# A top-k attention and two-layer MoE kernel: w3 @ w_out multiplied in float32 from decoded blocks, the order settled anew with later landings

## The chip, the cores and the metric

The kernel runs on 1 core of one Trainium2 chip. The metric is the device time in microseconds (us) of one execution. Engines are named as the profile names them: PE (TensorE; PEld its weight loads), DVE (VectorE), ACT (ScalarE), POOL (GpSimd), SP (SyncE, which issues the DMAs).

## The reference

```
# attention: q, k, v are (4, 8, 576, 64) float32, top_k = 32
scores = q @ k.T / 8
kth    = 32nd largest of each row; scores below it -> -1e9
attn   = exp(scores - max); attn /= sum(attn) + 1e-9
x      = (attn @ v), heads put side by side          # (2304, 512)
# moe: w_in (512, 2048), w_out (2048, 512)
h = x @ w_in;  x = (h * sigmoid(1.702 h)) @ w_out
# moe2: w1, w2 (512, 1024), w3 (1024, 1024), w_out (1024, 512)
out = ((x @ w1) * (x @ w2) @ w3) @ w_out             # (2304, 512) float32
```

The six weights reach the kernel as float64. Since nothing stands between `@ w3` and the last `@ w_out`, the kernel multiplies these two weights with each other once and applies the product, which it calls w34.

## The kernel before

The 2304 tokens are 18 tiles of 128; 18 tiles by 8 heads are 144 heads, counted here from 0.

**Weights (`weights`, L799).** A float64 weight arrives in 72 blocks of 128x512 elements (512 KB each). `load64` (L469) decodes each into a float32 block: one instruction on ACT or POOL for the low bits (L488 or L515), one for sign (L498 or L493), one on ACT into a PSUM bank (L503), one on DVE that joins them (L507). The landing buffer is free again when L503 has read it. `l2_scale` (L538) takes the norm of a group of blocks (four small matmuls per block, L551, and a few one-column instructions). `split` (L591) makes of a scaled block two float16 halves, hi and lo, since products are done as three float16 matmuls, hi*hi, hi*lo and lo*hi (`product_op`, L782: lines L789, L790, L791; 128x512 each).

**w34.** The moe2 w_out is 8 blocks (E4), w3 is 16 (E3). E4's blocks are split like others (hi: L598 ACT, L601 DVE or L604 POOL; lo: through PE L607 and DVE L614, through PE L610 and L611 and ACT L617, or on POOL L626 and L627). Each block of w3 is turned by PE and split by `split_turned` (L674), in one of two ways that the plan chooses: four float32 matmuls against a scaled identity (L681), hi on ACT (L691), a matmul that takes hi off the bank (L697), lo on ACT (L700); or four float32 transposes (L688), hi on ACT (L691), lo on DVE (L703). For each of the 8 output blocks then follow 24 float16 matmuls from two blocks of w3, and the result is itself split: hi L825 (ACT) or L828 (DVE), lo L832 (DVE) or L837 and L840.

**Tiles.** A head is a score matmul S (L1127), four rounds of MAX8 (L1147) and three of MATCH_REPLACE8 (L1150) on DVE, a cut out of PSUM (L1165) and an exponential (L1168) on ACT, a split into halves (ACT or POOL L1174, L1228; POOL L1177, L1180), a DMA transpose, and attn @ v on PE (L1195, L1199). A tile ends in the two MoE layers, which are products of `product_op` with the evictions between them. w34 is first used at the end of tile 0's MoE.

**Order.** Every step is an `Op` with one or more alternatives (engine, estimated cost). The order in which all ops are written, and the alternative of each, comes from a table, `PLAN`, found beforehand; `Order.run` (L76) goes through the ops in that order, gives each its buffers (pools of PSUM banks, SBUF blocks and slots) and records the instruction. So each engine's queue, SP's included, is fixed by the table, and each engine takes its queue strictly in order. The costs in the code (`lat=`, numbers beside "A", "V", "G", "T") are the estimates with which the table was found; they delay nothing on the chip.

Of the kernel before, what the change touches and what calls it, by code (L numbers as in the profile page):

```python
# [21 lines left out]
P = 128  # L22
C = 512
# [14 lines left out]
class Order:  # L38
    GAP = {"T": 0.25, "V": 0.16, "A": 0.16, "G": 0.1, "D": 0.05, "N": 0.0}
    SAME = {"T": 0.0, "V": 0.12, "A": 0.12, "G": 0.1, "D": 0.25, "N": 0.0}  # L40
    DMA = 2.1
    COLD = ((50.0, 1.28), (100.0, 1.03))
# [33 lines left out]
    def run(self, log=None):  # L76
        free = dict.fromkeys("TVAGD", 0.0)
        lock = moved = 0.0
        for o in sorted(self.ops, key=lambda o: o.rank):
# [21 lines left out]
            if e == "G" or (e == "V" and fn in self.both):  # L101
                cost += max(lock - now, 0.0)
                lock = now + cost
            o.eng, o.start = e, now
            free[e] = o.end = now + cost
            if e == "D":
                moved = max(moved, now + 0.3) + o.data
                o.end = max(o.end, moved) + o.lat
            for name, env, key in o.rel:
# [32 lines left out]
    'c-jq@W1A(t0!2$nC8?w;N!3{A^f^6k_t-N%wr$(CZQHhO+qP}%oqPYm{;;3D)>af%(G{rJN@^vG;`8~HJW5_AzhWpr!3t5h!jv>hCdKomQUXe>66Oo_rBgzb'  # L142
    'cqKteRthWCl{!iRUqN4zl3U5A6jLhu8u{Az+WAT<6@9yv`btA(lrmMB>-*)~9C9>dy0Th1t6WhYDKC|`zE{d`<&W}3`R6OBwpaQp!<CWB4CTJ>r*DLRoU&ZG'
    'p*&VzD_@l#itVrEpXiVG=T<MMoz#WuGIhDST0QJP;TIuK)lYt;2%l73CB2eX$>7WEi%_DJvPuPCC0}i&sZvxa?yI6yRaz+-m8`ySU!0Od(G=5X`KaP3)s&jP'
    'TE1pVS0$)K`l5X~l_E+<Wr%O6Z<exEX{~he4OYe~)0DbOJ*9!tMCqZ-QRXXqlmp5^rKd99w@^8*oKRXQEq&dULCR!hnX<vR$+uV8ubfoQD;JcD%4OxMa?O`j'
    '4Oe5;C&~-o2Srh#`d!gg<R@x6)l!+C`xDh1Y6-Qb+DL7owp7!oq5cRpuUbsaqQ>|W{JGS!YH_u^zn;H|+EgvAlvg?^os@1$FQvEAPZ^*LR7NOclnKgAWuvmC'
    '!J!668cZy>NLjD!R3<6sd{caveDeyfQPwK!l)D8#DxZ{Z%It#Ml*P(+Wu<aU*{s}FR`^ym*wJ8DgMG>|<&1J&xvAVy?kNwHhssmsx$;JNr@U8&s1wwc>Kb*e'
    'x=vlMZculthtyN*dG(t5Ks8mVW>N!coSIWr{YD|z@A>nn`P9;C8MU0MsaO?iDz%haM-BSJ)M$Spe`~da+D+}Fj#6v;>#Ftrjs5-Afoev-uaMs#;vcHcP?xAn'
    ')y-;Ge~&`F{bT*d)Jy7ob%nZBy`p|o|EQX#Ylim5|5p9%|LTv_qBNxO!ct48<<|;mr9vu(R1V3ig%{4IW!GA0Z8fa9nx_S{f!ZK#lr~<Qs+9|=rd1EA6*5;_'
    't<BVC7hbF_*S2a0wL{ti?U7bTYg4#`)>nI|ebzQ<I}7jC4roZnx~)5U27QmZ-+$15S-q-8soDJb)rx90wXNFD-&q~4PFMS?1JvQ_ICYkKR6Xv$qyANiHb@<;'  # L150
    'j#1~T^VCV|Wd9ETUiGxvOl|IO@9(H~QKzVj{2SGq>PPjgde{HT|3Uqw{#H%R3Q4O4wG3JoEli8ia%vCNcj`~o)*Nk^I?_L0y{_I+Q)wAPVzp!~ueLy2sI3Xv'
    'rk&Rwsn68s>I?Oys%WYPwbWX)mZ@;lM!rUq8<p0|Hfq?YNuxA{>kX<sXxN}cEl;DQMl~Cq)y`>`w9DER?Va{s`=}{8(RDp3;0E#q78O~puhKW`S@bwPR?ng5'
    '*GmRU1*!+0YrnML+JD+Vjq9GCUJvRqdP0!`fn0&wfuZ_ZeYU<%57l$)QF=i=LeHy5>P2*^r_wX(ne;F{Tu;=q={fa6dR@Jx-a+rASJfNpZS=PKM15mmQeab{'
    'T#@>L%7F%fP%R>)Q%F~>x7J+i9MUbMpEg08rp*bNAF@>2s1??VYIQ@}Y3;RqTA`34S_!R^R$ptN^$!`WjnPJEW3}laGqhP+cdduE=l{iF`VsAv_C@=vnfi9^'
    'SjerAXWAQWnYJQieaLR@q;^<49&$qarm6a4Ekq9lD(Thqi(2+TdA+9IT(75h)cXed=`;18TC+eeeXu@9Z?AXOyXal@Zh8;BzdleOrH|9c>l5^8`Ye5}K3`v~'
    'uh!S->-DYrZvBjYF>obtBk;ONY%nocDELax5KI@$8r-X&&=2S*^#^(`BiYDp9MMk)jt1@ruIYCIw*yZD--;MUMx&rn+Ncw(9jq5TR^*|6PJgM>lt{xd;*32-'
    '{slnL3cf2+ESM=+Hh8GWt;RPSKWf~^m|*lZCL2mh(V!hH9xSY<1R4bz>%H|?TD*Q%zpFpf%j&HHWArWhWqp7?Jg_0~RsW;=jOs>1qq)(}$ZTXWqKpzo1>>Wh'
    'BUm?B-)LmS80C$o!Olh(qn|O%m}<;578{L?iNQI>d}E8T$XF8G9^7H<G}ag!f*Xz9#vbF0@zcP7fk^PtaDfNXfb1X|WCJ-tE>IZc1^GgYf>NLY_@w{VRYNm`'
    'A&sCBW<(hAMowc?$_it&vB_v=bO^Qz_6jB$C5<9RDI<SMxnQMWm0(X}s4?6aX^b<b81syk#yVrGamjd|@-O9Oidyt~${XW_@!dFUJPh6qJ_;T-t^|(+uLbuT'
    '$Bc8vW#fi%&v<6MHr^XwjUUGE6a$z*fNv=PARs}OqTx-$n&ximFB%e>H8dhL36uooKxI%B)CCPd3(y9120cM9FboU_6TlvD1zZK+!8ULN90g~<U@!`d0W-iz'  # L160
    'FdfVR%fNE54y@3x>cmK8ECl<&NpKy!0B-?-Hsmlf%nHlETCgD;u1(Rp>m&53fsuhh!D+$&bQtUdc4+&w>)K82o_0UvPe|Ip+mLjD1S1HNL4HsG)C^q{>SnDE'
    '(q+vHr|UEHZTb%Vp#C{9FgQ3^E3{7NeW;qyw9L3L9+oOBb(n3sVUgxu^N@MgykuT8KZJb@`xJKFycrf@7BNei70ile<*-^|wZrP0EyFsR$IPeZEAzeiJxmKv'
    'D3PPYe`a#{4>JW-K@Ct3^eWtlU=fYbmhj%VFdB<4qlf4b`Vd~WWV@0Y<`L%+#x_oiE92G??IZd{B;n+UsW=fozzzu|QIV06MI(zxMw8W%`^kB7gWM!fB5y@1'
    'Q9Yx+M$)K$RuikMHO^XKowAlj@#y){ccVl!uv{z5O0r5=&7)dGjgLx>8Wgp}I%#F1L7GgfNAHe47X3cDI4v8!gl?rr=y7_UhQ-W^nIH3*K8e21Hq)mxD~n)p'
    'tXfR<m|ZcgSi6{ttS0No2C#uKW^Db~-m%Gc#n|okRi@asoz^a9SC4HHdoVU=uZ^ANEO3@MOPxc`vAE-Lr{b15C*s~XvAj4h$;<Id@y+8q#P^Nw!3W1*cCI`3'
# [24 lines left out]
    'BXM?|8<&iz5K$|l3GRiP;{kXC9)-u_X?Q38iGyT1o`aX*jU|`kJ@^aONlr2sAH>J;IeY@AA>~PP(u-Wcm+%dIyX15H83W>y#w3o!lLDkW=|cvP$z&#(MHZ07'  # L190
    'WG&f6j*tsvJ$XQ$l5gZ0c}Knz$I4`7vGQ7RR!*ykRn^);xRqd~SgowFR$Hr&HQU;3ZL@Y;pRMX<KXbS_Dr|Y!mavEBWV8gWMoZBSv>WX~d(m-p72QNH!oQ#&'
# [1376 lines left out]
```

## Time and profile before

| | before |
|---|---|
| device time, median of 3 | 990.6 us (990.5 to 991.75) |
| the profiled execution's own time | 994.35 us |
| its span, first to last instruction | 992.6 us |
| PE, DVE, ACT, POOL busy | 942.2, 901.7, 730.0, 832.5 us |
| mean granted TensorE clock | 0.988 of 2.4 GHz |

The profiled execution is 3.75 us above the median of the runs, and its span 2.0 us above. Spans and shares below are of the profiled execution. A matmul's record lasts from its issue to its modelled end, so records of matmuls that follow each other overlap, and PE's pace is read from the starts.

### The profile page before, as it was taken

The numbers are of one execution on the slowest core, as the hardware profiler recorded it, in microseconds if no ns is written. First come the engines' busy times: TensorE is split into PE (matmuls) and PEld (weight loads), VectorE is DVE, ScalarE is ACT, GpSimd is POOL, SyncE is SP. The second block draws the span as 40 slices with busy tenths as digits, with TensorE's granted clock in tenths as the row PEclk, the third lists the DMA queues.
The fourth block names the chain that finished last, engine by engine and source line by source line (L and its number), as shares of the span: only waits on it lengthen the run. The fifth ranks groups of instructions, "written<-read, shape, count | busy, mean of one in ns | idle before, by whom it ended". The sixth has DMA issues, their size and how long they took to land. (4 is left out here: it accounts for less than half of the span.)

```text
span 992.6 us, 20241 instructions
## 1 busy us (share of the span) xinstructions
PE 942.2 (95%) x6790; PEld 495.7 (50%) x6790; DVE 901.7 (91%) x1939; ACT 730.0 (74%) x1369; POOL 832.5 (84%) x1180
## 2 busy tenths in 40 slices
PE   5688879899999999999999999999999999999998
PEld 2445544445455555545555555545455555555544
DVE  6999999899999999999999999999999999999422
ACT  7999989896877787877688776776785775646241
POOL 6889999898899999999999999988897878757142
PEclk9699999999999999999999999999999999999999
DMA  9999988876788887767887868669666667555401
GB/s 322 291 280 291 277 179 191 173 135 131 122 149 151 155 156 136 134 130 152 146 158 139 147 129 147 121 127 165 127 126 134 113 118 117 111 90 102 99 11 33
DMA packets 398569, 149.37 MB, mean 150 GB/s; under 512 B 376576, under 2 KB 384768, under 8 KB 398464
## 3 DMA queue, kind: packets, MB, share of 16 engines
q1 hardware_dynamic: 398464, 148.07, 72.3%
q8 instruction: 53, 0.87, 0.4%
q14 instruction: 52, 0.43, 0.1%
HBM read 52.43 MB, written 4.72 MB: 58 GB/s over the span
## 5 line engine op out<-in xcount | busy, mean ns | idle before, releaser
L1147 DVE MAX8 m8s<-ysb 128x8 f32<-128x576 f32 x432 | 320.5, 752 | 5.7
L1150 DVE MATCH_REPLACE8 ysb<-m8s,ysb 128x576 f32<-128x576 f32 x288 | 213.6, 742 | 0.0
L1180 POOL TENSOR_TENSOR ysb<-ysb 128x512 f16<-128x512 f32 x141 | 163.8, 1166 | 0.3
L1165 ACT ACTIVATE ysb<-s_ps,m8s 128x576 f32<-128x576 f32 x144 | 106.7, 741 | 77.5 <-DVE m8s L1147 72.5
L789 PE MATMUL mm<-w,usb 128*128 128x512 f16 x388 | 147.1, 379 | 1.2 <-POOL usb L1319 1.0
L791 PE MATMUL mm<-w,usb 128*128 128x512 f16 x388 | 147.0, 379 | 0.0
L790 PE MATMUL mm<-w,usb 128*128 128x512 f16 x388 | 147.0, 379 | 0.0
L791 PEld LDWEIGHTS <-usb 128*128 128x128 f16 x912 | 89.1, 98 | 107.8
L789 PEld LDWEIGHTS <-usb 128*128 128x128 f16 x912 | 89.0, 98 | 100.2 <-issue 7.0
L1168 ACT ACTIVATE ysb<-ysb,nbs,asm 128x576 f32<-128x576 f32 x144 | 124.5, 867 | 17.0 <-DVE nbs L1157 8.5
L790 PEld LDWEIGHTS <-usb 128*128 128x128 f16 x912 | 89.1, 98 | 91.3 <-issue 2.1
L789 PE MATMUL mm<-wout,usb 128*128 128x512 f16 x304 | 115.3, 379 | 1.7 <-DMA usb<-usb 0.6
L791 PE MATMUL mm<-wout,usb 128*128 128x512 f16 x304 | 115.2, 379 | 0.0
L790 PE MATMUL mm<-wout,usb 128*128 128x512 f16 x304 | 115.2, 379 | 0.0
L1147 DVE MAX8 m8s<-s_ps 128x8 f32<-128x576 f32 x144 | 108.6, 754 | 6.2 <-PE s_ps L1127 3.4
L1150 DVE MATCH_REPLACE8 ysb<-m8s,s_ps 128x576 f32<-128x576 f32 x144 | 107.5, 747 | 0.0
L1127 PE MATMUL s_ps<-kts,qts 128*128 128x288 f16 (+1 forms) x640 | 96.4, 290 | 2.5 <-ACT ysb L1165 2.2
L789 PE MATMUL mm<-win,usb 128*128 128x512 f16 x220 | 83.5, 379 | 0.6 <-DMA usb<-usb 0.6
L791 PE MATMUL mm<-win,usb 128*128 128x512 f16 x220 | 83.4, 379 | 0.0
L790 PE MATMUL mm<-win,usb 128*128 128x512 f16 x220 | 83.4, 379 | 0.0
L1195 PE MATMUL mm<-v2s,ats 128*128 128x65 f16 (+1 forms) x1440 | 79.1, 194 | 3.4 <-DMA ats<-ysb 2.7
L1195 PEld LDWEIGHTS <-ats 128*128 128x128 f16 (+1 forms) x1440 | 73.5, 100 | 12.4 <-DMA ats<-ysb 3.8
(369 smaller groups left out, 2131.3 us busy)
## 6 DMA issues: line engine op xcount, KB each, us to landing
w<-in_moe_w_out_dram SPq DMA_DIRECT2D x24, 512.0 KB, 5.5
w<-in_moe_w_dram SPq DMA_DIRECT2D x22, 512.0 KB, 5.7
w<-in_moe_w_in_dram SPq DMA_DIRECT2D x16, 512.0 KB, 6.0
qts<-qts SPq DMA_DIRECT2D x34, 128.0 KB, 2.6
out_dram<-usb SPq DMA_DIRECT2D x17, 256.0 KB, 2.3
usb<-in_q_dram SPq DMA_DIRECT2D x15, 256.0 KB, 3.4
usb<-in_v_dram SPq DMA_DIRECT2D x11, 256.0 KB, 3.1
usb<-in_k_dram SPq DMA_DIRECT2D x10, 256.0 KB, 3.3
```

The lines of the kernel that those rows point to most:

```text
L789: nc.tensor.matmul(o, a[:, i, :], hi, start=(first and i == 0), stop=False)
L790: nc.tensor.matmul(o, a[:, i, :], lo, start=False, stop=False)
L791: nc.tensor.matmul(o, a[:, 4 + i, :], hi, start=False, stop=(last and i == 3))
L1127: nc.tensor.matmul(E["sp"][r : r + n, i], qe[q_][:, h, r : r + n], kt[:, j, i * HS : (i + 1) * HS], start=k_ == 0, stop=k_ == 1,)
L1147: nc.vector.max(out=E["m8"][:, 8 * i : 8 * i + 8], in_=E["sp"] if i == 0 else E["w"])
L1150: nc.vector.match_replace(out=two(E["w"]) if i == 0 else E["w"], in_to_replace=E["m8"][:, 8 * i : 8 * i + 8], in_values=E["sp"] if i == 0 ...
L1165: nc.scalar.activation(two(E["y"]), E["sp"], AF.Prelu, bias=E["m8"][:, TOPK - 1 : TOPK], scale=-1.0, alpha=1.0 / FAR)
L1168: nc.scalar.activation(E["y"], E["y"], AF.Exp, bias=E["nb"], scale=nesc)
L1180: return lambda: eng.tensor_tensor(hl()[:, S + SR : 2 * S], E["y"][:, 0:SM], hl()[:, 0:SM], op=ALU.subtract)
L1195: nc.tensor.matmul(heads_av()[r : r + n, j_, 0 : D + 1], at_, v2[:, j_, blk, D : P + 1], start=(i == 0), stop=(i == 8),)
```

## The change

Three parts.

1. E4's 8 blocks are no longer split, and the 16 blocks of w3 no longer halved. A block of w3 is turned by four float32 transposes and copied from PSUM to SBUF as float32 (`turned3`); w34 is 8 float32 matmuls of 128x512 per output block, 64 in all, straight from decoded blocks. The scales, which were in the halves, go into the eviction of the result (`by`, two columns of a new `s34`).
2. The split of w34's result has the scale as a column, and its lo may be made on POOL.
3. The estimates in the planner are changed: DMA landings later (`lat=`), POOL instructions a little dearer, a price for DVE instructions that share with POOL, and a limit on DMA work under way at a DMA transpose. A new `PLAN` was found with them: the order and the alternatives of the whole program are others.

```diff
+    def turned3(W, E):
+        bank = lambda: E["mm"]
         def f_in():
-            E["by"] = -1.0
-            for i in range(4):
-                nc.tensor.matmul(
-                    bank()[:, i], W["w"][:, i * P : (i + 1) * P], turned, start=i == 0, stop=False, skip_group_check=True
-                )
...
+            for i in range(0, C, P):
+                nc.tensor.transpose(E["mm"][:, i : i + P], W["w"][:, i : i + P], ident)
+        def f_a():
+            nc.scalar.copy(E["f"], E["mm"])
...
+        a = pe(0.45, 0.0, f_in, deps=[W["join"], W["gram"]], env=E, acq=["f", "mm"], rel=[("blk", W, "w")], tag="w3 in")
+        return op([("A", 0.48, f_a, 0.0), ("V", 0.6, f_v, 0.0)], 0.0, deps=[a], env=E, rel=["mm"], tag="w3 turned")
...
-        i4, s4, d4 = l2_scale(E4, quarter(0))
-        sp4 = [split(E, s4, d4) for E in E4]
-        g3 = [l2_scale(E3[8 * g : 8 * g + 8], quarter(1 + g)) for g in range(2)]
+        i4, s4, d4 = l2_scale(E4)
+        g3 = [l2_scale(E3[8 * g : 8 * g + 8]) for g in range(2)]
+        s34 = wcols(2)
...
-                tr = split_turned(W, g3[f // 4][1], e)
-                last = product_op(
-                    0.0, lambda E=E: E["mm"], lambda e=e: e["t"], E4, [4 * kc + i for i in range(4)],
-                    kc == 0, kc == 1, [tr, last, pr] + sp4[4 * kc : 4 * kc + 4], [("mm", E, "mm")] if kc == 0 else [], rel, "w34",
-                )
+                tr = turned3(E3[2 * f + kc], e)
+                for i in (0, 2):
+                    def f_w34(E=E, e=e, i=i, kc=kc):
+                        for n in (i, i + 1):
+                            nc.tensor.matmul(
+                                E["mm"], e["f"][:, n * P : (n + 1) * P], E4[4 * kc + n]["w"],
+                                start=kc == 0 and n == 0, stop=kc == 1 and n == 3,
+                            )
...
-                nc.scalar.activation(halves(E["o"])[0], E["mm"], AF.Copy, scale=G34)
+                nc.scalar.activation(halves(E["o"])[0], E["mm"], AF.Copy, scale=by)
...
-        ld = dma(0.5, due - 20, f_load, env=E, acq=keys, tag="w load", lat=2.5, data=1.62)
+        ld = dma(0.5, due - 20, f_load, env=E, acq=keys, tag="w load", lat=2.9, data=1.62)
...
-            tr = [dma(1.35, due + 8, f_t, deps=[lo], env=E, acq=["at"], rel=["hl"], tag="a T", lat=1.6, data=1.42, after=last_of.get("a T"))]
+            tr = [dma(1.35, due + 8, f_t, deps=[lo], env=E, acq=["at"], rel=["hl"], tag="a T", lat=2.2, data=1.42, after=last_of.get("a T"))]
```

PE's queue where w3 is first turned. Names: `mm` are PSUM banks, `wout` and `win` hold decoded weight blocks here, `usb` the halves or copies of turned w3, `s_ps` the scores. Before, behind the S of head 3:

```order
L688 MATMUL mm_96<-ident,wout 128x128 x4
L681 MATMUL mm_97<-tsb,wout 128x128 x4
L681 MATMUL mm_95<-tsb,wout 128x128 x4
L697 LDWEIGHTS ident
L697 MATMUL mm_97<-usb,ident 128x512
L688 MATMUL mm_96<-ident,wout 128x128 x4
L697 LDWEIGHTS ident
L697 MATMUL mm_95<-usb,ident 128x512
L688 MATMUL mm_97<-ident,wout 128x128 x4
L789 LDWEIGHTS usb
L789 MATMUL mm_95<-wout,usb 128x512
```

In the changed kernel the first float32 products (L815), just ahead of the S of head 4, with the transposes (L690) of a later block between them (`wout` and the `w_` tiles are blocks of E4 and E3):

```order
L815 MATMUL mm_94<-w_71,usb 128x512 x2
L690 MATMUL mm_93<-ident,wout 128x128 x4
L577 LDWEIGHTS ones
L577 MATMUL mm_95<-wsm,ones 128x1
L994 LDWEIGHTS ones
L994 MATMUL mm_96<-kvc,ones 128x1
L995 LDWEIGHTS ones
L995 MATMUL mm_96<-kvc,ones 128x1
L815 MATMUL mm_94<-w_71,usb 128x512
L815 MATMUL mm_94<-wout,usb 128x512
L815 MATMUL mm_94<-w_70,usb 128x512 x2
```

The take-off matmuls L697 are gone, products come in long float32 matmuls, and other work of PE stands between those of one output block.

ACT's queue at the same stage, before (L691 and L700 are hi and lo of w3, L503 and L498 decode later blocks, L1168 is a head's exponential):

```order
L691 ACTIVATE usb<-mm_96,wsm 128x512
L1168 ACTIVATE ysb<-ysb,nbs,asm 128x576
L691 ACTIVATE usb<-mm_97 128x512
L503 ACTIVATE mm_98<-w_72 128x512
L691 ACTIVATE usb<-mm_95 128x512
L700 ACTIVATE usb<-mm_97 128x512
L691 ACTIVATE usb<-mm_96,wsm 128x512
L700 ACTIVATE usb<-mm_95 128x512
L498 ACTIVATE win<-w_72 128x512
```

and in the changed kernel (L693 is the copy of a turned block; L513, L508, L498 decode; L1174, L1180 and L1171 are a head's exponential, hi and cut):

```order
L1174 ACTIVATE ysb<-ysb,nbs,asm 128x576
L693 COPY usb<-mm_94 128x512
L990 ACTIVATE usb,kvc<-wout,nbs 128x8x64
L991 ACTIVATE kr_82,kvc<-rest,nbs 64x2x64
L693 COPY usb<-mm_93 128x512
L693 COPY usb<-mm_96 128x512
L513 ACTIVATE mm_96<-w_70 128x512
L420 ACTIVATE usb<-wout,kvc 128x8x64
L1180 CAST ysb<-ysb 128x576
```

One copy per block stands where one or two instructions stood.

## Rows read from the trace of the kernel before

**Rows 1.** The page: busy us of each engine, share, instructions.
```profile
PE 942.2 (95%) x6790; PEld 495.7 (50%) x6790; DVE 901.7 (91%) x1939; ACT 730.0 (74%) x1369; POOL 832.5 (84%) x1180
```

**Rows 2.** Windows: us, busy of each engine, granted clock, DMA share, GB/s.
```profile
core 0: us, PE busy (x) PEld busy (x) DVE busy (x) ACT busy (x) POOL busy (x), PEclk, DMA share, GB/s
0.00:200.00 200.00, 161.09 (x1109) 90.36 (x1110) 181.28 (x412) 183.68 (x352) 176.39 (x264) 0.94 0.93 251
200.00:225.00 25.00, 24.02 (x169) 12.31 (x169) 25.00 (x62) 23.50 (x45) 22.78 (x34) 1.00 0.71 130
225.00:992.60 767.60, 757.08 (x5515) 393.07 (x5512) 695.44 (x1467) 522.86 (x974) 633.36 (x884) 1.00 0.68 125
```

**Rows 3.** The same view in stretches of 25 us.
```profile
25.00:50.00 25.00, 16.14 (x107) 11.02 (x105) 24.06 (x57) 22.85 (x48) 21.67 (x32) 0.67 1.00 291
50.00:75.00 25.00, 21.90 (x136) 11.80 (x135) 24.17 (x50) 24.41 (x45) 22.04 (x33) 1.00 0.94 281
75.00:100.00 25.00, 22.76 (x162) 13.78 (x162) 24.93 (x56) 25.00 (x46) 23.43 (x35) 1.00 1.00 292
100.00:125.00 25.00, 21.85 (x175) 13.03 (x173) 23.75 (x54) 24.09 (x48) 23.96 (x35) 1.00 1.06 274
```

**Rows 4.** Waits of the DMA queue (SP), 50 to 100 us, then 100 to 200 us.
```profile
SPq L483 <- ACT mm L503: 17.3, 14, 3.7
...
SPq L483 <- ACT mm L503: 15.0, 9, 3.9
```

**Rows 5.** PE's timeline: start us, us, instruction.
```profile
43.93 0.60 PE L688 MATMUL mm<-ident,wout 128*128 128x128 f32 x4
45.20 2.02 PE L681 MATMUL mm<-tsb,wout 128*128 128x128 f32 x16 [0.66 <-POOL nbs L1157]
...
50.67 0.38 PE L789 MATMUL mm<-wout,usb 128*128 128x512 f16 x1 [0.40 <-ACT usb L700]
50.88 0.38 PE L790 MATMUL mm<-wout,usb 128*128 128x512 f16 x1
51.10 0.38 PE L791 MATMUL mm<-wout,usb 128*128 128x512 f16 x1
...
212.79 1.02 PE L652 MATMUL mm<-win,tsb 128*128 128x512 f32 x2
213.64 1.02 PE L652 MATMUL mm<-w,tsb 128*128 128x512 f32 x2
...
225.08 0.65 PE L1127 MATMUL s_ps<-kts,qts 128*128 128x288 f16 x4
```

**Rows 6.** Groups of ACT, then DVE: shapes, count | busy us, mean ns.
```profile
L1464 ACT COPY usb<-mm 128x512 f32<-128x512 f32 x25 | 14.4, 577 | 10.6 <-PE mm L791 10.3 <-POOL usb L1319 0.3
L700 ACT ACTIVATE usb<-mm 128x512 f16<-128x512 f32 x9 | 5.5, 613 | 0.0
L691 ACT ACTIVATE usb<-mm 128x512 f16<-128x512 f32 x9 | 5.4, 620 | 0.0
L691 ACT ACTIVATE usb<-mm,wsm 128x512 f16<-128x512 f32 x7 | 4.9, 693 | 0.0
...
L703 DVE SCALAR_TENSOR_TENSOR usb<-mm,wsm,usb 128x512 f16<-128x512 f32 x7 | 5.1, 733 | 0.0
L832 DVE SCALAR_TENSOR_TENSOR win<-mm,win 128x512 f16<-128x512 f32 x3 | 2.0, 673 | 0.0
```

**Rows 7.** Single lines up to 75 us, E4's splits: min/median/max ns.
```profile
L601 DVE TENSOR_SCALAR wout<-w,wsm x1: 1077/1077/1077, 32.5 to 32.5; 128x512 f16<-128x512 f32 x1
...
L604 POOL TENSOR_SCALAR wout<-w,wsm x3: 694/697/698, 30.1 to 31.8; 128x512 f16<-128x512 f32 x3
...
L614 DVE SCALAR_TENSOR_TENSOR wout<-w,wsm,mm x4: 730/734/747, 34.2 to 41.5; 128x512 f16<-128x512 f32 x4
...
L627 POOL TENSOR_TENSOR wout<-w,wout x2: 1159/1162/1165, 34.9 to 36.9; 128x512 f16<-128x512 f32 x2
```

**Rows 8.** One line of ACT in the first 45 us, the same columns.
```profile
L598 ACT ACTIVATE wout<-w,wsm x3: 710/712/722, 29.2 to 33.3; 128x512 f16<-128x512 f32 x3
```

More of the change, by code (lines that the diff above doesn't have):

```diff
@@ L101, in run @@
             if e == "G" or (e == "V" and fn in self.both):
-                cost += max(lock - now, 0.0)
+                cost += max(lock - now, 0.0) + (self.TWO if e == "V" else 0.0)
                 lock = now + cost
@@ L106, in run @@
             if e == "D":
+                units = self.UNITS.get(o.tag, 1024)
+                if o.tag[-2:] == " T":
+                    under = units
+                    for land, n in flight[:-13:-1]:
+                        under += n
+                        if under > self.ROOM:
+                            free[e] = o.end = max(o.end, land)
+                            break
                 moved = max(moved, now + 0.3) + o.data
                 o.end = max(o.end, moved) + o.lat
+                flight.append((o.end, units))
             for name, env, key in o.rel:
@@ L243 @@
+    'y}dqOKd-+x$QztCGHs|g#2c14+#BJIN}S+L@kV=N5+{0-6DN67y=mSIZ>IM@x71ei'
 )
@@ L588, in l2_scale @@
             return inv, sc, c
-        return inv, (turned, pool(0.35, due - 40, f_turn, deps=[c] + list(free), tag="w turn"), sc), c
+        return inv, (turned, pool(0.38, due - 40, f_turn, deps=[c] + list(free), tag="w turn"), sc), c
     def split(E, sc, dep, bank=False):
@@ L802, in weights @@
         E3 = [load64(rows(w3, f, kc)) for f in range(8) for kc in range(2)]
-        i4, s4, d4 = l2_scale(E4, quarter(0))
-        sp4 = [split(E, s4, d4) for E in E4]
-        g3 = [l2_scale(E3[8 * g : 8 * g + 8], quarter(1 + g)) for g in range(2)]
-        pr = None
+        i4, s4, d4 = l2_scale(E4)
+        g3 = [l2_scale(E3[8 * g : 8 * g + 8]) for g in range(2)]
+        s34 = wcols(2)
+        d34 = [
+            dve(
+                0.09, 0.0, lambda g=g: nc.vector.tensor_scalar(s34[:, g : g + 1], g3[g][1], s4, G34, op0=ALU.mult, op1=ALU.mult),
+                deps=[d4, g3[g][2]], tag="w34 scale",
+            )
+            for g in range(2)
+        ]
+        last = None
         ready["w34"] = []
@@ L810, in weights @@
             E = {}
-            last = None
+            by = s34[:, f // 4 : f // 4 + 1]
             for kc in range(2):
                 e = {}
-                W = E3[2 * f + kc]
-                tr = split_turned(W, g3[f // 4][1], e)
-                rel = [("t", e, "t")] + ([("blk", w, "o") for w in E4] if f == 7 and kc == 1 else [])
-                last = product_op(
-                    0.0, lambda E=E: E["mm"], lambda e=e: e["t"], E4, [4 * kc + i for i in range(4)],
-                    kc == 0, kc == 1, [tr, last, pr] + sp4[4 * kc : 4 * kc + 4], [("mm", E, "mm")] if kc == 0 else [], rel, "w34",
-                )
@@ L836, in f_less34 @@
-            def f_less34(E=E):
-                nc.tensor.matmul(E["mm"], nid, halves(E["o"])[0], start=False, stop=True, skip_group_check=True)
-            def f_lo34_a(E=E):
-                nc.scalar.activation(halves(E["o"])[1], E["mm"], AF.Copy, scale=G34)
-            l34 = op([("N", 0.0, None, 0.0), ("T", 0.24, f_less34, 0.0)], 0.0, deps=[h34], tag="w34 pre")
+                tr = turned3(E3[2 * f + kc], e)
[5 more added lines that the diff above has]
+                                start=kc == 0 and n == 0, stop=kc == 1 and n == 3,
+                            )
+                    w4_ = [E4[4 * kc + n]["join"] for n in (i, i + 1)]
+                    rel = [("f", e, "f")] if i else []
+                    if f == 7 and kc == 1 and i:
+                        w4_ = w4_ + [E4[7]["gram"]]
+                        rel = rel + [("blk", w, "w") for w in E4]
+                    last = pe(
+                        1.72, 0.0, f_w34, deps=[tr, last] + w4_, env=E if not i else None,
+                        acq=[("mm", E, "mm")] if kc == 0 and not i else [], rel=[(n_, k_, v_) for n_, k_, v_ in rel], tag="w34",
+                    )
@@ new lines, in weights, with f_hi34, f_hi34_v, f_lo34 @@
+            H34.append(E)
+            def f_hi34(E=E, by=by):
+                nc.scalar.activation(halves(E["o"])[0], E["mm"], AF.Copy, scale=by)
+            def f_hi34_v(E=E, by=by):
+                nc.vector.tensor_scalar(halves(E["o"])[0], E["mm"], by, None, op0=ALU.mult)
+            def f_lo34(E=E, by=by):
+                hi, lo = halves(E["o"])
+                nc.vector.scalar_tensor_tensor(lo, E["mm"], by, hi, op0=ALU.mult, op1=ALU.subtract)
+            h34 = op([("A", 0.49, f_hi34, 0.0), ("V", 0.59, f_hi34_v, 0.0)], 0.0, deps=[last, d34[f // 4]], env=E, acq=[("blk", E, "o")], tag="w34 hi")
@@ L850, in weights @@
         for j in range(NG):
-            used = (E4, E3[0:8], E3[8:16])
-            turn = (quarter((3 + j) % 4), [E["in"] for E in used[j - 1]] if j else [])
-            _, s_, d_ = l2_scale(H_in[4 * j : 4 * j + 4], *turn, inv=iin[:, j : j + 1])
+            _, s_, d_ = l2_scale(H_in[4 * j : 4 * j + 4], quarter((3 + j) % 4), inv=iin[:, j : j + 1])
             ready["win"] += [split(E, s_, d_) for E in H_in[4 * j : 4 * j + 4]]
@@ L1321, in hi_lo @@
         a = op([("A", 0.515, h_a, 0.0), ("V", 0.37, od.two(h_v), wait_hi)], due, deps=deps, env=E, acq=["h"], tag=tag + "hi")
[L1322 removed]
+        return op([("G", 1.13, l(nc.gpsimd), 0.0), ("V", 0.66, od.two(l(nc.vector)), wait)], due, deps=[a], env=E, rel=rel, tag=tag + "lo")
     def moe(t, X):
```

287 lines of the change are left out of this document (133 added, 154 removed).

## The prediction

> **What bounds the kernel now.** I read the page first. PE is busy 95% of the span, DVE 91%, POOL 84%, ACT 74% [rows 1], which would make PE the engine to spare. Then the windows, because such shares are means over stages. They show two kernels in one. Up to 200 us DVE, ACT and POOL are busy 181.3, 183.7 and 176.4 us, about 90% each, while PE has records in 161.1 us only: 38.9 us of it are empty. From 225 us on it is the other way round: PE has 757.1 of 767.6 us filled, with 10.5 us empty, DVE 695.4, POOL 633.4, ACT 522.9 [rows 2]. So the first 200 us are set by the three engines that decode and split weights beside the first heads, and the rest by PE. The windows of 25 us say the same of the stretch in which w3 is worked on: ACT 24.4 and 25.0 of 25, DVE 24.2 and 24.9, PE 21.9 and 22.8 [rows 3].
>
> The empty part of PE is larger than it looks. Products that follow each other start 0.215 us apart (50.67, 50.88, 51.10), yet each record is 0.38 us long [rows 5], so a record covers up to 0.16 us behind its own work. The Trainium skill says this in "Perfetto Trace Analysis", section Identifying the Most-Contended Engine: the busy share of matmuls is no good measure of how near PE is to its limit, since they are pipelined. The trace agrees (0.38 beside 0.215). By the busy share alone any PE time added here would be paid in full; by the stage it is not.
>
> DMA is the fourth candidate of the early stage: its share is 0.94 to 1.06 from 25 to 125 us [rows 3]. But the weight loads themselves wait in SP's queue for L503 on ACT, which frees a landing buffer: 17.3 us between 50 and 100 us and 15.0 us from 100 to 200 us [rows 4]. Decoding paces the loads more than the loads pace decoding.
>
> **PE's share of the change.** Removed: 8 x 24 = 192 float16 products at 0.215 = 41.3 us; 36 float32 matmuls of 128x128 (L681; 16 records, two for each, in 2.02 us with the last one's end, so 0.22 each) = 8.0; 28 transposes, at most 0.60/4 = 0.15 each, taken at 0.11 like one record of L681 = 3.1; nine L697 and one L837 at 0.215 = 2.1; E4's lo through PE (five L607, one L610 with L611) = 6 x 0.215 + 0.85 = 2.1. Together 56.6. Added: 64 float32 products of 128x512, 0.85 each (212.79 to 213.64) = 54.4 [rows 5], and 64 transposes at 0.11 = 7.0, together 61.4. Net +4.8 us, all of it in the stage where PE has 38.9 us empty. That cover is the reason to cost it at nothing; if it is not there when the work comes, the price is 4.8 us.
>
> **The other three engines.** E4's eight hi were three on ACT at 0.71 [rows 8], one on DVE at 1.08, four on POOL at 0.70; its eight lo five on DVE at 0.73, one on ACT, two on POOL at 0.70 + 1.16 [rows 7]. For w3's sixteen blocks ACT did sixteen hi (nine at 0.62, seven at 0.69) and nine lo at 0.61, DVE seven lo at 0.73; now ACT does sixteen copies out of PSUM, of which the nearest row is L1464 at 0.58 [rows 6]. For w34's eight results DVE keeps its lo but with a scale in a column (priced as L703, 0.73, instead of 0.67), ACT seven hi at 0.69 instead of 0.60 [rows 6]. POOL also loses three scalings of the identity and one constant, 128 columns each, which I bound between 0.17 and 0.70 by L604 and take at 0.35.
> ACT: removed 2.1 + 0.6 + 10.4 + 5.5 + 4.2 + 0.6 = 23.4, added 9.2 + 4.8 = 14.0: -9.4. DVE: removed 3.7 + 1.1 + 5.1 + 4.7 + 0.7 = 15.3, added 5.9 + 0.7 + two columns at 0.2: -8.3. POOL: -2.8 - 3.7 - 1.4 = -7.9. Sum -25.6 us, and nearly even: 8.5 for each of the three engines that set the stage.
>
> Two things shorten the chain besides: a turned block goes to its products after one eviction instead of hi, L697 and lo, and the turn no longer waits for the norms.
>
> **What the new order does with it.** The order of the two programs, counted by instructions, tells where the work stands. On PE 5,513 matmuls stand behind the S of head 24 before and 5,508 now; behind that of head 40 it is 4,814 in both, the same in every kind. So nothing is moved out of or into the PE-bound part: the end moves by what head 24 moves, which today starts at 225.08 us [rows 5], plus whatever changes in PE's 10.5 empty us. On DVE 394 instructions stand ahead of head 24's first MAX8 before and 382 now; the differences are seven L703 and six L614 gone and little else. S of head 4 stands behind the products of w34's first output block in both programs, before behind six of the second's too.
> Each of the three engines is filled to 90% in that stage, so 8.5 us less work on each brings head 24 forward by 8.5 x 0.9 = 7.6 us if the empty tenth stays. Ends of this term: nothing (what is freed only becomes idle time) and 9.4 (ACT alone sets the stage and closes up). I take 7.5.
>
> The later landings alone cost or save nothing by themselves; they moved instructions. I take 0 for that and keep half of PE's 10.5 us as its bound on the gaining side, and 5 us, as much the other way, on the losing side.
>
> **Sum.** 992.6 - 7.5 = 985.1 us of span in a profile; the median of the runs lies 2.0 us under the profiled span, so 983 us for the median, against 990.6.
>
> **Rivals.**
> A, PE pays (slower). PE takes its queue in order, and a float32 pair blocks it for 1.7 us. If the products come while an S waits behind them, PE's empty time is not where the new work is: the 38.9 us are many short waits. Then head 24 comes 4.8 us later and the other engines' relief turns into waiting: 990.6 + 4.8 = 995.4. It decides when PE's empty time up to 200 us stays at 38.9 us or over. Against it: the stage's engines are the other three, and each is relieved.
> B, transfers pace the stage (same). If the DMA share near 1.0 is the true limit, 72 blocks land when they land and all else waits: 990.6. For it: the share of 1.06. Against it: SP's waits for L503.
> C, the order gains more (faster). With landings that come when the table expects them, half of PE's empty 10.5 us behind 225 us goes as well: 983 - 5 = 978.
> D, the clock (same). Between 25 and 50 us the granted clock is 0.67 in the mean, so it stood at half, 1.2 GHz, for a good part; in the two windows behind, which hold transposes of w3 too, it is 1.00 [rows 3]. If it fell in the new stage, the eight float32 products of one output block would cost 6.8 us more, which eats the gain: about 990. The Trainium skill would expect it sooner with transposes ("TensorE: Matmul & The Clock Gate", section Part 4: PE-mode transpose: they do not count as PE-busy in the way matmuls do). The 28 transposes here ran without a fall, and the long products stand next to them, so I give it little.
>
> **How the numbers follow.** A change of 0.2% (2 us) is about what runs of this kernel can tell from none. Forecast (980 to 988) 0.55, C 0.18, B 0.11, D 0.03, A 0.13. Faster: 0.55 + 0.18 = 0.73; same: 0.11 + 0.03 = 0.14; slower: 0.13. The predicted time is the forecast's 983. The range leaves out A and the far end of C: low is 983.1 less another 1.9 (ACT's bound of 9.4 instead of 7.5) and C's 5, so 976; high is B's 990.6, so 991. The forecast's own range is 980 to 988.
>
> **What would show it.** In the new profile: float32 products of w34 0.85 us apart; PE's filled time up to 200 us near 166 us or above; ACT, DVE and POOL still at about 90% there; head 24's S near 217.5 us; from there to the end 767 us again. Wrong if head 24 starts at 225 us or later (A or B: by A PE without gaps between 45 and 125 us, by B ACT with new waits for weight landings), or if head 24 comes early and the rest takes longer than 770 us, which would be the new order's fault.

## The result and the profile after

The changed kernel takes 980.27 us (median of 4 runs, 979.02 to 984.21) against 990.93 of the kernel before beside it: ratio 0.9898, 95% interval 0.9868 to 0.9928, so 10.1 us faster on 990.6. The forecast was 983 us, with a range of 976 to 991. The profiled execution takes 981.0 us, its span is 979.2 us, the mean granted clock 0.998.

The lines of the changed kernel are numbered otherwise: S is L1133, attn @ v L1201, `product_op` L779 to L781, the float32 products are L815 and the turns L690. The page after, in the columns of [rows 1]:

```profile
PE 940.6 (96%) x6674; PEld 495.3 (51%) x6674; DVE 890.3 (91%) x1918; ACT 724.4 (74%) x1361; POOL 821.2 (84%) x1179
```

PE, which the shares name as the engine to spare, has hardly less to do (942.2 to 940.6). The windows after, first those of [rows 2], then the two parts that meet at the S of head 24:

```profile
core 0: us, PE busy (x) PEld busy (x) DVE busy (x) ACT busy (x) POOL busy (x), PEclk, DMA share, GB/s
0.00:200.00 200.00, 169.24 (x1041) 93.97 (x1042) 182.79 (x421) 187.50 (x356) 175.04 (x268) 0.99 0.93 258
200.00:225.00 25.00, 24.39 (x191) 12.63 (x189) 24.96 (x62) 22.47 (x42) 20.46 (x31) 1.00 0.70 125
225.00:979.20 754.20, 746.95 (x5448) 388.69 (x5445) 682.55 (x1437) 514.47 (x965) 625.67 (x882) 1.00 0.69 126
...
0.00:216.68 216.68, 185.51 (x1166) 102.24 (x1167) 199.47 (x463) 202.61 (x384) 188.25 (x287) 0.99 0.92 248
216.68:979.20 762.52, 755.07 (x5510) 393.06 (x5508) 690.84 (x1456) 521.83 (x979) 632.92 (x893) 1.00 0.68 126
```

The same two parts of the kernel before, whose head 24 starts at 225.08 us:

```profile
0.00:225.08 225.08, 185.18 (x1278) 102.67 (x1278) 206.35 (x474) 207.25 (x396) 199.25 (x298) 0.95 0.90 238
225.08:992.60 767.52, 757.00 (x5514) 393.07 (x5512) 695.36 (x1467) 522.77 (x974) 633.28 (x884) 1.00 0.68 125
```

Ahead of head 24 PE is busy for the same 185 us; DVE has 6.9 us less to do, ACT 4.6, POOL 11.0: 22.5 together, 7.5 each. In these two executions head 24 starts 8.4 us earlier. Up to 200 us PE's empty time fell from 38.9 to 30.8 us, the three others stay at about 90% (88 to 94%). That looks like the forecast. Behind head 24, where no change was forecast, nearly the same work (one float32 product in place of six float16 ones) takes 762.5 us instead of 767.5. The two make 13.4 us between the profiled executions; before's lies 3.4 us above its median and the changed kernel's 0.7 above its own, so between medians it is 10.7. The excess of before's execution lies ahead of head 24, since five other kernels in its order take no less time behind it (see "Behind head 24" below). So between medians some 4 us were gained ahead of head 24, and not 8.4.

The stretches of [rows 3] after:

```profile
25.00:50.00 25.00, 19.21 (x117) 13.94 (x118) 22.14 (x56) 22.85 (x48) 21.68 (x37) 1.00 1.10 283
50.00:75.00 25.00, 23.30 (x115) 12.47 (x114) 24.76 (x56) 24.46 (x44) 21.91 (x32) 1.00 0.92 278
75.00:100.00 25.00, 22.45 (x105) 11.74 (x104) 23.07 (x51) 23.18 (x43) 21.36 (x35) 1.00 0.99 295
100.00:125.00 25.00, 24.71 (x170) 13.94 (x169) 24.76 (x63) 24.93 (x46) 23.57 (x33) 1.00 0.99 286
```

PE is fuller in three of the four, and the granted clock is 1.00 in all of them, between 25 and 50 us too, where it was 0.67. PE's timeline answers to [rows 5]:

```profile
53.64 1.88 PE L815 MATMUL mm<-w,usb 128*128 128x512 f32 x4
55.35 1.02 PE L815 MATMUL mm<-wout,usb 128*128 128x512 f32 x2
56.21 3.60 PE L815 MATMUL mm<-w,usb 128*128 128x512 f32 x8
59.65 1.04 PE L690 MATMUL mm<-ident,wout 128*128 128x128 f32 x8
60.52 0.65 PE L1133 MATMUL s_ps<-kts,qts 128*128 128x288 f16 x4
...
216.68 0.65 PE L1133 MATMUL s_ps<-kts,qts 128*128 128x288 f16 x4
```

A float32 product is two records: four records go from 53.64 to 55.35, so 0.855 us for a product (forecast 0.85), and eight transposes from 59.65 to 60.52, 0.109 each (0.11). The score matmuls of a head stand behind the turns of two blocks. The evictions, each with the least, the median and the longest time in ns, answer to [rows 6]:

```profile
L693 ACT COPY usb<-mm x16: 558/575/612, 37.3 to 108.6; 128x512 f32<-128x512 f32 x16
L832 ACT ACTIVATE win<-mm,wsm x3: 655/675/687, 54.0 to 111.0; 128x512 f16<-128x512 f32 x3
L839 DVE SCALAR_TENSOR_TENSOR win<-mm,wsm,win x3: 734/743/745, 56.0 to 113.2; 128x512 f16<-128x512 f32 x3
```

All sixteen copies are on ACT at 0.575 (forecast 0.58); hi and lo of w34 take 0.675 and 0.74 (0.69, 0.73). SP still waits for ACT's eviction before it issues a weight load (50 to 100 us, then 100 to 200 us, as [rows 4]):

```profile
SPq L493 <- ACT mm L513: 15.1, 10, 5.1
...
SPq L493 <- ACT mm L513: 17.2, 11, 4.6
```

32.3 us before, 32.3 after. And what PE waits for behind head 24, first before, then after:

```profile
PE mm L1195 <- DMA ats<-ysb: 1.8, 5, 0.6
PE s_ps L1127 <- ACT ysb L1165: 1.3, 4, 0.5
PE mm L789 <- DMA usb<-usb: 1.2, 2, 0.6
PE mm L789 <- POOL usb L1319: 1.0, 1, 1.0
PE mm L789 <- DMA tsb<-usb: 0.8, 2, 0.6
PE mm L789 <- ACT usb L1353: 0.2, 1, 0.2
```

```profile
PE s_ps L1133 <- ACT ysb L1171: 1.4, 5, 0.4
PE mm L779 <- DMA usb<-usb: 1.1, 2, 0.7
PE mm L779 <- DMA tsb<-usb: 0.4, 1, 0.4
PE mm L1201 <- DVE xsb L1260: 0.2, 1, 0.2
```

6.3 us became 3.1: the waits of attn @ v (L1195) for a transposed attention block are gone, and so is that of a product (L789) for POOL. The windows say the same in total: 10.5 empty us of PE before, 7.45 after. That is 3 of the 5 us; counted from start to start, beyond the usual distance for each kind of matmul, PE's pauses fell by 4.3 us (17.8 to 13.5).

### The profile page after: what moved, and what is told of

Same layout as the page of the kernel before. It is cut to its first block, busy times and chain, and to the rows that moved or that the text cites. A ratio compares the mean times of both kernels' runs of the same rounds, so it can differ in the third digit from the quotient of the medians.

```text
span 979.2 us, 19984 instructions
## 1 busy us (share of the span) xinstructions
PE 940.6 (96%) x6674; PEld 495.3 (51%) x6674; DVE 890.3 (91%) x1918; ACT 724.4 (74%) x1361; POOL 821.2 (84%) x1179
## 2 busy tenths in 40 slices
DMA packets 398568, 149.35 MB, mean 153 GB/s; under 512 B 376576, under 2 KB 384768, under 8 KB 398464
## 5 line engine op out<-in xcount | busy, mean ns | idle before, releaser
L1171 ACT ACTIVATE ysb<-s_ps,m8s 128x576 f32<-128x576 f32 x144 | 106.4, 739 | 76.0 <-DVE m8s L1153 62.4
L779 PE MATMUL mm<-w,usb 128*128 128x512 f16 x367 | 139.1, 379 | 1.2 <-DMA usb<-usb 1.1
L781 PE MATMUL mm<-w,usb 128*128 128x512 f16 x367 | 139.1, 379 | 0.0
L780 PE MATMUL mm<-w,usb 128*128 128x512 f16 x367 | 139.1, 379 | 0.0
L1174 ACT ACTIVATE ysb<-ysb,nbs,asm 128x576 f32<-128x576 f32 x144 | 123.8, 865 | 18.8 <-POOL nbs L1163 11.2
L781 PEld LDWEIGHTS <-usb 128*128 128x128 f16 x800 | 78.3, 98 | 94.4
L779 PEld LDWEIGHTS <-usb 128*128 128x128 f16 x800 | 78.2, 98 | 85.1 <-issue 2.9
L780 PEld LDWEIGHTS <-usb 128*128 128x128 f16 x800 | 78.3, 98 | 80.6 <-issue 0.7
L1133 PE MATMUL s_ps<-kts,qts 128*128 128x288 f16 (+1 forms) x640 | 96.0, 290 | 4.0 <-DMA qts<-qts 2.4
L779 PE MATMUL mm<-wout,usb 128*128 128x512 f16 x220 | 83.5, 379 | 0.1
L781 PE MATMUL mm<-wout,usb 128*128 128x512 f16 x220 | 83.4, 379 | 0.0
L780 PE MATMUL mm<-wout,usb 128*128 128x512 f16 x220 | 83.4, 379 | 0.0
L779 PE MATMUL mm<-win,usb 128*128 128x512 f16 x213 | 80.8, 379 | 0.0
L781 PE MATMUL mm<-win,usb 128*128 128x512 f16 x213 | 80.7, 379 | 0.0
L780 PE MATMUL mm<-win,usb 128*128 128x512 f16 x213 | 80.7, 379 | 0.0
L1325 POOL TENSOR_TENSOR usb<-usb 128x512 f16<-128x512 f32 x60 | 69.5, 1159 | 12.6 <-ACT usb L1319 9.5
L1201 PEld LDWEIGHTS <-ats 128*128 128x128 f16 (+1 forms) x1440 | 73.6, 101 | 11.0 <-issue 5.9
```

The costliest lines, as they stand in the source:

```text
L779: nc.tensor.matmul(o, a[:, i, :], hi, start=(first and i == 0), stop=False)
L780: nc.tensor.matmul(o, a[:, i, :], lo, start=False, stop=False)
L781: nc.tensor.matmul(o, a[:, 4 + i, :], hi, start=False, stop=(last and i == 3))
L1133: nc.tensor.matmul(E["sp"][r : r + n, i], qe[q_][:, h, r : r + n], kt[:, j, i * HS : (i + 1) * HS], start=k_ == 0, stop=k_ == 1,)
L1171: nc.scalar.activation(two(E["y"]), E["sp"], AF.Prelu, bias=E["m8"][:, TOPK - 1 : TOPK], scale=-1.0, alpha=1.0 / FAR)
L1174: nc.scalar.activation(E["y"], E["y"], AF.Exp, bias=E["nb"], scale=nesc)
```

## The experiments

Five questions. Does the relief of DVE, ACT and POOL set the time (R), does the new order (O), does PE pay (P), do transfers pace the stage (D)? And once the first answers were there: why does the same arithmetic fail in the old order? Each kernel ran beside the kernel before, whose median was 990.25 to 991.98 us on these chips; so kernels are compared by their ratio to it, and a difference of 0.001 is 1 us. The 95% intervals reach 1.1 to 2.3 us to either side, and 3 us for the changed kernel itself (4 runs). "Order" stands for the whole new table, the choice of engines included; no run takes the two apart.

**The old order with the new arithmetic.** In the kernel before, its table untouched, E4 isn't split, w3 is turned and copied once, and 64 float32 products take the places of the float16 ones; instructions that are gone leave no gap in a queue.

```diff
-                last = product_op(
-                    0.0, lambda E=E: E["mm"], lambda e=e: e["t"], E4, [4 * kc + i for i in range(4)],
...
+                    for n in (i, i + 1):
+                        nc.tensor.matmul(
+                            E["mm"], e["f32"][:, n * P : (n + 1) * P], E4[4 * kc + n]["w"],
...
-            nc.scalar.activation(E["t"][:, 0:4], bank(), AF.Copy, scale=E["by"])
+            nc.scalar.copy(E["f32"], E["mm"])
```

> The order of before, step by step, with the float32 products of the change in it: E4 is not split, w3 is turned by transposes and copied once, w34 is 64 float32 products. Theory R (relief: the early stage is set by DVE, ACT and POOL, and each loses some 8 us of work): most of the gain without any new order, 982 to 986 us, head 24's S near 218 us, and 767 us from there to the end as before. Theory O (the new order, found with later landings, made the gain): 989 us or over, head 24 at 224 us or later. Theory P (the added 4.8 us of PE are paid): near 995 us.

995.35 us (9 runs), ratio 1.0040 (1.0026 to 1.0053): slower than before. R alone is refuted; the times of O and of P both fit. The windows from 50 to 150 us of before, of this kernel and of the changed one:

```profile
50.00:150.00 100.00, 85.88 (x656) 50.47 (x655) 95.53 (x214) 95.08 (x178) 93.16 (x136) 0.98 0.95 256
```

```profile
50.00:150.00 100.00, 90.29 (x550) 50.39 (x549) 91.49 (x207) 89.65 (x166) 90.79 (x132) 0.98 0.96 254
```

```profile
50.00:150.00 100.00, 91.91 (x559) 50.58 (x558) 95.64 (x219) 96.06 (x179) 90.69 (x134) 0.98 0.96 270
```

In the old order DVE falls from 95.5 to 91.5 and ACT from 95.1 to 89.7: the relief is there and has become idle time. In the new order both are full again. The longest waits in the old order between 60 and 130 us, ACT's, then PE's and SP's (in this kernel L819 are the products, L1207 is attn @ v):

```profile
ACT win L837 <- PE mm L819: 3.3, 1, 3.3
ACT xsb L1263 <- PE mm L1207: 2.2, 1, 2.2
...
PE mm L1207 <- DVE win L845: 2.8, 1, 2.8
...
SPq L1195 <- PE mm L1207: 8.1, 2, 5.5
```

The eviction of w34 (L837) waits for the products (L819), attn @ v (L1207) for w34's lo (L845), the next attention transpose (L1195) for attn @ v. In all ACT waits 9.5 us for PE there, 5.1 of them for the products; in the kernel before it is 0.3. SP's wait for attn @ v is not new: it is 6.2 us in the kernel before, in the same stretch.

**The work given back in the new order.** At each of the sixteen turns of w3 ACT does an idle instruction, at the first eleven DVE and POOL do too (tiles that are not used at that time).

```diff
+            nc.scalar.activation(idle[0], idle[0], AF.Copy, scale=1.0)
+            if n < 11:
+                nc.vector.scalar_tensor_tensor(idle[1], idle[1], 1.0, idle[1], op0=ALU.mult, op1=ALU.max)
+                nc.gpsimd.tensor_scalar(idle[2], idle[2], 1.0, 1.0, op0=ALU.mult, op1=ALU.mult)
```

> The changed kernel with idle work beside the turns of w3, about what the change took away: 16 ACT instructions of 128x512 (0.63 us each, 10 us), 11 on DVE (0.74, 8.1 us), 11 on POOL (0.70, 7.7 us), on buffers that nothing else uses then. Theory R: the gain of the early stage goes, plus 6 to 9 us over the changed kernel, 986 to 989 us. Theory O: plus 2 us at most, 980 to 982 us.

985.93 us (6 runs), ratio 0.9958 (0.9942 to 0.9975): 5.9 us of the 10.1 are lost again, 4.2 stay, which is the lower end of R and rules out O alone. By the two intervals the 5.9 are good to some 3.4 us. Groups of the idle work:

```profile
L697 ACT ACTIVATE psb<-psb 128x512 f32<-128x512 f32 x16 | 10.0, 626 | 0.1
L699 DVE SCALAR_TENSOR_TENSOR psb<-psb 128x512 f32<-128x512 f32 x11 | 9.7, 885 | 0.1
L700 POOL TENSOR_SCALAR tsb<-tsb 128x512 f32<-128x512 f32 x11 | 7.5, 686 | 0.2
```

27.2 us, 9.1 for each engine (somewhat more than was taken away), cost 5.9: 0.65 us of time for one of mean load, where the prediction took 0.9. With the interval of the 5.9 the two are barely told apart. Then ACT's part alone (the first line of the diff) and DVE's alone (the third):

> The changed kernel with idle work on ScalarE alone: one 128x512 instruction, some 0.58 us, beside each of the sixteen turns of w3 (9.3 us in all), about what the change took from it; VectorE and GpSimd stay relieved. All three together cost 5.7 us. Theory A (ScalarE sets the early stage, so its load alone counts): 4.5 us or more, 985 us or above. Theory M (the three share the stage, none alone sets it): 1 to 3 us, 982 to 984 us. If ScalarE has slack: within 1 us of 980.3.

> The changed kernel with idle work on VectorE alone: eleven 128x512 instructions of some 0.73 us (8.0 us in all) beside the first eleven turns of w3; ScalarE and GpSimd stay relieved. Theory A (ScalarE sets the early stage): within 1 us of 980.3. Theory M (the three share it): 1 to 3 us, 982 to 984 us. If VectorE sets it, 4.5 us or more: 985 us or above.

983.95 and 982.71 us (6 runs each), both at the ratio 0.9919 (0.9904 to 0.9933, and 0.9901 to 0.9938), so 2.1 us for either, with an uncertainty as large. Theory M fits best: none sets the stage alone. From 50 to 150 us ACT is at 99.88 of 100 us in the one, DVE at 99.36 in the other.

**More and less on PE.** Eight products more (one for each output block), and in another kernel every second of the 64 left out:

```diff
+                        if kc == 0 and i == 0:
+                            nc.tensor.matmul(E["mm"], e["f"][:, 0:P], E4[0]["w"], start=True, stop=True)
```

```diff
-                        for n in (i, i + 1):
+                        for n in (i,):
```

> The changed kernel with the first float32 product of each output block issued twice: 8 more, 6.8 us more PE work in the early stage. Theory R (PE's early empty time covers it): plus 0 to 2 us, 980 to 982 us. Theory P (PE's work is paid in full there): plus 6.8 us, 987 us.

> The changed kernel with every second of the 64 float32 products of w34 left out (32 x 0.85 = 27.2 us less on TensorE in the early stage; half of the terms of w34 are left out of what is computed). Theory R (TensorE's share of the early stage is covered): within 1.5 us of 980.3, as eight products more moved nothing. Theory K (the products are on the path, as links of a chain from a turned block to the eviction of w34): 4 us or more faster, 976 us or less.

980.92 us (ratio 0.9899, 0.9883 to 0.9916) and 980.57 us (0.9895, 0.9874 to 0.9915): 6.8 us more or 27.2 us less on PE move nothing. The windows of the second, 50 to 150 us:

```profile
50.00:150.00 100.00, 76.56 (x507) 42.76 (x508) 96.68 (x221) 97.19 (x182) 91.55 (x134) 0.91 1.00 273
```

PE is empty for 23 of 100 us, and the granted clock falls (0.91 instead of 0.98); DVE and ACT are about where they were. So PE's share of the stage is covered in the new order, as the prediction said.

**Half the bytes of the weights.** Behind the first sixteen, loads of the common landing buffers bring half a block (46 of 72 in the changed kernel, 12.1 MB less by the pages, 149.35 to 137.29); the same in the kernel before.

```diff
-            nc.sync.dma_start(raw().bitcast(U32), src.bitcast(U32))
+            nload[0] += 1
+            k = C if kind == "raw" and nload[0] > 16 else 2 * C
+            nc.sync.dma_start(raw().bitcast(U32)[:, 0:k], src.bitcast(U32)[:, 0:k])
```

> The changed kernel with 46 of the 72 weight loads at half their size, 11.8 MB less; the other half of those blocks is left as it was in the buffer, so part of the weights is left out. All instructions and their order stay. Theory R (decoding sets the pace, not the transfers): within 3 us of the changed kernel, 977 to 982 us. Theory D (transfers pace the early stage): at the 290 GB/s of the stage 11.8 MB are 40 us of transfer, of which at least 10 come off, 970 us or less.

> The kernel before, untouched but for this: behind the first sixteen, each weight load of the common landing buffers brings only the first half of its block (the rest of the block is whatever lay in the buffer, so part of the weights is left out of what is computed). Every instruction and every wait stays. Theory L (landings pace the early stage of either kernel alike): the same 4.5 us or more that the changed kernel won by it, so 986 us or less. Theory E (before the change the decoding engines set the stage, and transfers come to the fore only when those are relieved): 988 us or more, a gain of at most 2.5 us.

The changed kernel: 975.8 us (4 runs), ratio 0.9855 (0.9835 to 0.9875), 4.3 us less, which is more than R allows (977 us) and far less than D asks for (970). Before: 989.38 (9 runs), 0.9975 (0.9964 to 0.9986), 2.5 us less, theory E at its edge. The changed kernel's windows, 50 to 150 us:

```profile
50.00:150.00 100.00, 94.10 (x586) 51.93 (x587) 98.92 (x231) 99.78 (x186) 94.11 (x139) 1.00 0.73 180
```

With a DMA share of 0.73 instead of 0.96 ACT rises from 96.06 to 99.78 and DVE from 95.64 to 98.92. So transfers have a part in keeping the last 4% of the stage empty; they don't set it.

**Why the old order loses.** The old order with float32 products, with half loads (diff as above), with every second product left out, and with both:

> The order of before with float32 products (995.4 us), and the same halved weight loads (part of the weights is left out of what is computed). Theory T (in the old order what the change frees is lost to waits for weight landings, of which GpSimd alone shows some 17 us): most of what the old order lost comes back, 8 us or more, so 987 us or less, near the changed kernel's 981. Theory Q (it is lost in TensorE's queue, to long float32 products and turns that stand ahead of scores and norms, and to the clock): no more than the 4.5 us that the changed kernel won by halved loads, so 990 us or more.

> The order of before with float32 products (995.4 us; halved weight loads won 3.8 us of it), and every second of the 64 products left out (27.2 us less on TensorE; half of the terms of w34 are left out of what is computed). Theory Q (in the old order the long products stand in TensorE's queue ahead of scores and norms, and of the evictions of w34 for which ScalarE and VectorE wait, and that eats what the change freed): 8 us or more come back, 987 us or less. Theory S (the fixed places of the other engines' instructions eat it, whatever TensorE does): a gain of at most 3 us, 992 us or above.

> The order of before with float32 products, with halved weight loads and with every second float32 product left out (part of the weights and half of w34's terms are left out of what is computed); the one alone took 3.8 us off 995.4, the other 4.2. Theory S (the rest of the loss is the order itself: each engine's queue has its instructions at places that suited the former work): the two add up, about 987 us, and 986 at the least, still some 11 us above the changed kernel with halved loads (975.8), where fewer products moved nothing. Theory C (transfers and products cover for each other, so that either alone shows only a part): 981 us or less. If the two win the same time: 990 us or more.

991.59 us (1.0001, 0.9989 to 1.0014), 991.14 us (0.9997, 0.9984 to 1.0009) and 987.85 us (0.9961, 0.9947 to 0.9974). Of 1.0040 either takes about 4 us, both together 7.8: they add up, and neither T nor Q is the whole. In the old order half of the products cost 4.3 us; in the new one the same half cost nothing that shows (0.3, within the interval). And with both reliefs it is still 10.5 us above the changed kernel with half loads alone (0.9961 against 0.9855): theory S, the order itself. 5.9 of the 10.5 us lie behind head 24 (769.3 against 763.4). The windows with both reliefs, 50 to 150 us:

```profile
50.00:150.00 100.00, 74.71 (x497) 42.55 (x496) 94.76 (x212) 91.97 (x171) 94.62 (x138) 0.90 0.72 165
```

PE and DMA have room, and ACT still has only 91.97: its instructions wait in their places, 4.5 us for PE, 2.1 for DVE and 1.0 for POOL. The changed kernel with half loads has no such wait of ACT in this stretch.

**The estimates without the order.** The changed kernel with before's estimates in the planner and the new table: every queue is the same, only buffers differ.

```diff
-    ROOM = 2600
+    ROOM = 10**9
-    TWO = 0.25
+    TWO = 0.0
...
-        ld = dma(0.5, due - 20, f_load, env=E, acq=keys, tag="w load", lat=2.9, data=1.62)
+        ld = dma(0.5, due - 20, f_load, env=E, acq=keys, tag="w load", lat=2.5, data=1.62)
```

> The changed kernel, its table and so its order untouched, but with the planner's estimates of before (landings 0.3 to 0.6 us earlier, no limit on DMA work under way, GpSimd cheaper, nothing for VectorE's sharing). Each engine gets the same instructions in the same order; only the buffers (banks, blocks, slots) that they get differ. Theory N (the estimates act through the order that was found with them and not by themselves): within 1.5 us of 980.3. Theory B (estimates nearer to the chip choose buffers that are free in time, and that is worth something): 983 us or more.

980.98 us (6 runs), 0.9893 (0.987 to 0.9916): no difference that shows. What the later landings do, they do through the order found with them.

**Behind head 24.** From the S of head 24 to the end, the profiles of six kernels in before's order have 767.5 (before itself), 768.8, 769.2, 769.0, 769.6 and 769.3 us, of eight in the new order 762.5, 763.3, 761.5, 763.4, 762.9, 763.4, 762.5 and 763.3, whatever was done ahead of it. The order is worth 6.0 us there (means 768.9 and 762.9). One kernel of each order, the kernel before with half loads and the changed one with the work given back, up to the S of head 24 and from there:

```profile
0.00:218.64 218.64, 181.19 (x1278) 100.88 (x1279) 205.29 (x474) 206.00 (x396) 199.05 (x298) 0.96 0.75 190
218.64:987.90 769.26, 757.57 (x5514) 393.40 (x5512) 695.24 (x1467) 522.84 (x974) 633.13 (x884) 1.00 0.68 125
```

```profile
0.00:220.70 220.70, 187.81 (x1166) 100.72 (x1166) 208.24 (x477) 210.21 (x400) 198.50 (x298) 0.98 0.91 243
220.70:984.00 763.30, 754.98 (x5510) 393.08 (x5508) 690.90 (x1456) 522.19 (x979) 632.87 (x893) 1.00 0.69 125
```

With the work given back head 24 starts later than in the kernel before with half loads, which is only 2.5 us faster than the kernel before, and the whole is still 3.9 us shorter (spans of 984.0 and 987.9). What the parts of the change are worth ahead of head 24 follows by subtraction (an estimate: the ratios, less the 6.0 us behind it where the order is new; good to about 1.5 us, the last to 3). The arithmetic in the old order: 4.0 us slower. The new order with the work given back: 1.8 us slower. Both together: 4.1 us faster, and the three kernels that differ from it without a change in time (0.9893 to 0.9899) say the same. Neither part gains there without the other.

## Why the prediction was right, and where not

The time was forecast 2.7 us too long, inside the range, on the right side. That it came so close is in part luck: the forecast put 7.5 us ahead of head 24 and nothing behind it, and the runs put some 4 us ahead and 6 behind, so two misses of opposite sign went into one sum. By its steps:

- **What bounds.** Right: two kernels in one. 27.2 us less on PE in the first part are worth nothing that shows, 27.2 us more on the three others cost 5.9.
- **PE's share.** Right in its sizes (0.855 and 0.109) and in its cover; but the cover belongs to the new order. In the old order one half of the products is worth 4.3 us: PE takes its queue in order, and the evictions and attn @ v behind the products wait. That the old order came out at 995.35, close to rival A's 995.4, is in part chance, since half of the loads are worth as much there (3.9 us).
- **The other three.** Sizes right. The busy time ahead of head 24 fell by 22.5 us (forecast 25.6, -9.4 ACT, -8.3 DVE, -7.9 POOL); it is spread otherwise (4.6, 6.9, 11.0), since the new table gave ACT other work.
- **From relief to time.** The mis-sized term: "8.5 us less work on each brings head 24 forward by 8.5 x 0.9 = 7.6 us if the empty tenth stays". Between medians head 24 comes some 4 us earlier. By the idle work it is 0.65 for one of mean load, so 5.5 for the 8.5, and the new order takes part of that back ahead of head 24. The empty part need not stay in proportion (read from the windows, not shown by a run of its own): from 50 to 150 us ACT and DVE had some 4 us of slack, which takes up part of what is added (up to 99.88 of 100), and transfers hold part of what is freed (4.3 us back with half loads).
- **The order.** The step that failed: "The later landings alone cost or save nothing by themselves; they moved instructions. I take 0 for that". The first half is right (before's estimates change nothing), the 0 isn't: the order is worth 4.2 us over the whole span when the work is given back, and 6.0 behind head 24. That matmuls stand behind head 24 in the same number told where the work is, and not whether PE waits there: its waits fell from 6.3 to 3.1 us, and that stretch from 768.9 to 762.9 in the mean. Rival C, with 5 us, described this; it came together with a smaller term for the relief. Of the two signs, "767 us again" was wrong (762.5). Head 24 at 217.5 us (216.7) came true by luck: it was counted from the 225.08 us of before's profile, which was 3.4 us slower than before's median.
- **B** as stated is refuted, since the time fell; that transfers pace the stage in part is shown (4.3 us). **D** is refuted for the changed kernel: the granted clock is 1.00 in all four stretches that hold float32 products and transposes. The Trainium skill's "TensorE: Matmul & The Clock Gate", section Part 4: PE-mode transpose, says that transposes don't count as PE-busy in the same way; with 64 of them between long products the granted clock stayed at 1.00. That the 0.67 between 25 and 50 us is gone does not explain the gain either: of 20 runs of the kernel before, the 8 with a mean clock of 0.997 or more took 991.7 us on average, the 12 with 0.991 or less 991.9.

The float32 product takes 0.855 us against 0.215 of a float16 one, 3.98 times. The Trainium skill's "FP8 and Floating Point Precision", section TensorE Precision Notes, has true FP32 as four passes, and the trace agrees.

What stays open: which places in the order are worth how much, behind head 24 above all, and how much of it is the new choice of engines; and what the shorter chain of a turned block is worth by itself, since the idle work gave back load and not its links. That was not tried.

## What to carry to other kernels

When queues are fixed, arithmetic and order are one change: cheaper arithmetic in the old order was 0.4% slower, in an order found for it 1.0% faster, and the order without the relief already 0.4% faster. Load taken off several engines that share a stage can be worth less than its mean (0.65 here, with a wide interval). A stretch read from one execution of each kernel carries that execution's chance: 8.4 us ahead of head 24 in the two profiles were some 4 between medians, and the kernels of the same order told which part was chance. Instruction counts on each side of a point show that hardly any work moved past it; that the waits there stay is a further claim, to be bounded by the stalls in that stretch.

## What the runs showed of the hardware

In the changed kernel the clock did not fall under float32: with all 64 products and 64 transposes between 25 and 125 us the granted clock was 1.00, 2.4 GHz. Other runs with the same 64 products do show a fall: 0.93 in the mean from 75 to 100 us in the old order (PE busy 20.14 of 25 us) and in the kernel with before's estimates (21.69). With half of the products gone in the new order its mean from 50 to 150 us was 0.91, so it stood at 1.2 GHz for some 18 of 100 us, with PE busy 76.56 us of the 100 instead of 91.91. The time did not rise with it (ratio 0.9895 against 0.9898).
